# Two attention steps and a gated layer on one core: the first batch cut in seven chunks instead of eight, its 320-column chunk taken into the running maximum last, and a new instruction order

## The chip, the cores and the metric

The kernel runs on one core of one Trainium2 chip. The metric is the device time of one execution in microseconds (us). It was timed in 3 runs; the profile is of one more execution.

## What is computed

The input `x` has 4 batches of 12800 rows of 128 numbers. 32 inducing rows `I` first attend to `x`, which gives 32 rows `h` for each batch; then every row of `x` attends to `h`. The result goes through a causal convolution of 5 taps, whose sigmoid gates a linear map of it, and a second linear map.

```python
def mab(q, kv):
    s = scale * (q @ kv.transpose(0, 2, 1))
    s = s - s.max(-1, keepdims=True)
    a = np.exp(s)
    a /= a.sum(-1, keepdims=True) + 1e-09
    return a @ kv
h = mab(I, x)
attn = mab(x, h)
...
for k in range(K):                       # K = 5
    gate_pre += conv_w[k][None, None, :] * xp[:, k:k + S, :]
gate = 1.0 / (1.0 + np.exp(-gate_pre))
val = x @ w_val                          # x is attn here
return (gate * val @ w_out)
```

## The kernel before

The 12800 rows of a batch lie as 4 strips of 3200, and each strip is cut in chunks (`SIZES`), so that a chunk of 480 columns stands for 4 x 480 rows. A batch goes through two halves.

In the first half each chunk's scores against `I` are made (`s1`, L298, on PE) and moved to SBUF with their maximum (`e1`, L303, DVE). The maxima are merged in groups (`GROUPS`): `gm` (L320) reduces them, `ng` merges the four strips with five small operations (L335 and four of L337, on POOL or DVE), and `f` (L328, ACT) is the factor by which the older sums are scaled when the maximum has grown. Then the chunk's scores are exponentiated (`x1`, L345, ACT) and transposed (`tr`, L348, DVE), and PE adds them up against the rows of `x` (`h`, L362). DVE adds those sums (`ha`, L374 to L378) to `H`, and at the end PE and DVE turn `H` into `hT`, the 32 rows `h` (`hh`, L394 and L395; `hT`, L402 to L404).

`h` needs the rows of `x` in another layout (`xk`). For the later batches they are loaded; in the first batch most chunks (`MADE`) make them on the chip instead, by transposes on PE (`tp`, L272) that DVE or ACT copy to SBUF (`tpev`, L280 or L278).

The second half starts at `hT`. Its rows are folded into the weights of the gate and of the values (`g0` to `g3`, `wf`, `wt`, `W`; L412 to L472). A chunk is scored against `hT` (`s2`, L512, PE), transposed (`tin`, L516, DVE), and its softmax made: maximum (`mx`, L526, DVE), subtraction (`sub`, L531, POOL), exponential (`ex`, L537, ACT), sum and reciprocal (`sm`, L543 to L548, DVE), product (`nm`, L554, POOL), transposed back (`tout`, L557, DVE) and split in a high and a low half of 16 bits (`phi`, L560, ACT; `plo`, L562, POOL). Chunks that stand together in `JOINT` share these steps.

Then comes the `visit` of the chunk: PE's matmuls of 32 rows, four strips at once, 15 of the gate (L579) and 3 of the values (L586) for each strip. ACT takes the tanh (`th`, L671), DVE multiplies gate and values (`gv`, L680), ACT and POOL split the product in two halves of 16 bits (`hi`, L686, into a buffer `gh`; `lo`, L688, into a buffer `gl`), PE makes the output from these halves (`o`, L714, three matmuls for each of four strips), ACT or DVE move it to SBUF (`ev`, L726 or L728) and SP stores it. In the last chunk the output is made from 32-bit numbers.

What runs where and when is written out in three tables: `ORDER` lists all operations, each engine takes its own in that order, `SLOTS` gives each its buffer or PSUM bank, and `ENGINES` picks the engine of those that may run on two. The numbers next to an operation in the code (the costs) do not reach the chip; they are what the tables were once searched with. An engine runs in order, so an operation that waits holds all behind it.

`b`, `c`, `p` in a name are batch, chunk and pair of strips: `gv.0.1.0` is the first pair of chunk 1 of batch 0.

Of the kernel before, what the change touches and what calls it, by code (L numbers as in the profile page):

```python
# [35 lines left out]
SIZES = [[128, 256, 480, 480, 480, 480, 480, 416]] + [[448, 448, 448, 448, 448, 480, 480]] * 2 + [[448, 480, 480, 480, 480, 480, 352]]  # L36
XB = 15
JOINED = [[1], [], [], []]
CUTS = {(0, 2): [(0, 8), (8, 7)]}
MADE = {(0, 0): [], (0, 1): [], (0, 2): [], (0, 3): [], (0, 4): [], (0, 5): [], (0, 7): []}  # L40
GROUPS = [[[2, 3], [4, 5], [6, 7], [1, 0]]] + [[[0, 1, 2, 3], [4, 5, 6]]] * 3
HSUMS = [[[2, 3], [4, 5], [6, 7], [1, 0]]] + [[[0], [1], [2], [3], [4], [5], [6]]] * 3
JOINT = [[[0], [1], [2], [3], [4], [5], [6, 7]]] + [[[0], [1, 2], [3, 4], [5, 6]]] * 3
# [3 lines left out]
BUFS = dict(xt=10, xk=4, ss=5, et=3, e=2, pt=1, tg=4, gh=3, gl=2, os=4, H=2, z=3, m2=3, W=2, w2=2, wf=2, wo=2, wof=1, hT=2)  # L47
ASIDE = {(0, 0): 'os2', (0, 7): 'os2'}
# [46 lines left out]
def tile_kernel(ctx: ExitStack, tc: tile.TileContext, xt, xk, indT_in, w64, out):  # L95
# [7 lines left out]
    op = plan.op  # L103
# [4 lines left out]
    def tile_of(name, shape, dt=F32):  # L108
# [4 lines left out]
                  e=([P, 2 * XB, M], F32), pt=([P, 2 * CW], F32), tg=([P, 2, CW], F32), gh=([P, 2, CW], F16),  # L113
                  gl=([P, 2, CW], F16), os=([P, 2, CW], F32), H=([P, P + 1], F32), z=([P, 4, 32], F32),
# [14 lines left out]
        u=1, osc=1).items()} for b in range(B)]  # L129
# [182 lines left out]
    def group(b, g):  # L312
# [13 lines left out]
        op(("ng", b, g), ("POOL", "DVE"), f, dict(POOL=1.7, DVE=0.65), [("e1", b, cs[0]) if one else ("gm", b, g)])  # L326
        if g:
            op(("f", b, g), "ACT", lambda: S.activation(sm["f"][:, g:g + 1], sm["ng"][:, g - 1:g], AF.Exp, bias=sm["ng"][:, g:g + 1],  # L328
                                                        scale=-1.0), 0.22, [("ng", b, g), ("ng", b, g - 1)])
# [58 lines left out]
    def prep(b):  # L388
# [17 lines left out]
        op(("hT", b), "DVE", f_n, 0.62, [("hh", b)], [hT], [key])  # L406
# [42 lines left out]
        op(("g3", b), "DVE", g3, 0.48, [("g2", b), ("whi", b)], [], [pv, w2])  # L449
# [38 lines left out]
        op(("u", b), ("POOL", "DVE"), o1, dict(POOL=2.0, DVE=0.78), [("qm", b)])  # L488
# [318 lines left out]
def run_plan(tc, plan, slot):  # L807
# [173 lines left out]
```

## Time and profile before

| what | value |
| --- | --- |
| median of 3 runs (lowest, highest) | 277.88 us (277.62 to 278.01) |
| the profiled execution, its own time | 278.09 us |
| its span, first to last instruction | 276.3 us |
| PE busy (matmuls) | 263.6 us, 95% |
| DVE, ACT, POOL busy | 216.2, 202.0, 199.9 us |
| granted clock of PE | 1.000 of full speed |
| chain that ended last: PE, DVE, POOL | 72%, 14%, 6% of the span |

The profiled execution is 0.21 us above the median. PE is busy nearly all the time, but busy says only that a matmul is open; how dense its work is must be read from the rows of single stretches. The chain is followed back from the last instruction, each time to what released it.

### The profile page before, as it was taken

Reading aid. Unit: us, or ns where it says so; the run is one execution under the profiler, and the core shown is the slowest. Engines: PE = TensorE matmul, PEld = TensorE weight load, DVE = VectorE, ACT = ScalarE, POOL = GpSimd, SP = SyncE. Lnnn points to the kernel's source line nnn. Section 1 sums busy time; section 2 is a strip of 40 time slices with the busy share of each in tenths; the row PEclk is TensorE's granted clock in tenths of the full one; section 3 lists DMA queues with packets and bytes.
Section 4 is the critical chain, followed back from the end, with each engine's and each line's share of the span. In section 5 each row is a group of like instructions: output and inputs, shape, how many; then the busy total and the mean of one; then the engine's idle time right before and its main releaser. Section 6 shows DMA issues by size and latency. Waiting matters only on the chain.

```text
span 276.3 us, 10610 instructions
## 1 busy us (share of the span) xinstructions
PE 263.6 (95%) x4569; PEld 146.5 (53%) x4569; DVE 216.2 (78%) x455; ACT 202.0 (73%) x259; POOL 199.9 (72%) x182
## 2 busy tenths in 40 slices
PE   8999898798999999999999999999999999999993
PEld 4558336474444555665565476565445555444451
DVE  0669999997997999998786899887898953645561
ACT  2538257665568888676988685997598899997752
POOL 1002158766889948677998769999999999996650
PEclk9999999999999999999999999999999999999999
DMA  7999999679989599999996799443331443333466
GB/s 268 423 414 420 414 386 354 254 266 421 375 295 332 179 321 334 342 345 362 407 354 215 278 327 365 187 163 125 134 138 66 161 180 147 140 140 142 156 228 224
DMA packets 23631, 74.49 MB, mean 270 GB/s; under 512 B 1952, under 2 KB 16800, under 8 KB 23584
## 3 DMA queue, kind: packets, MB, share of 16 engines
q1 hardware_dynamic: 23440, 73.79, 71.4%
q8 instruction: 36, 0.59, 0.8%
q14 instruction: 11, 0.09, 0.1%
q10 hardware_dynamic: 144, 0.02, 0.0%
HBM read 47.58 MB, written 26.21 MB: 267 GB/s over the span
## 4 chain that ended last, share of the span: by engine, by line
PE 72%; DVE 14%; POOL 6%; issue 4%; ACT 2%; POOLq 0%; DVEq 0%; ACTq 0%
PE banks L579 24%; PE banks L714 21%; PE banks L362 7%; PE banks L298 5%; PE banks L586 5%; PE banks L512 5%; POOL gl L688 3%; DVE tg L680 2%; PE banks L272 2%; DVE ss L303 2%; PE banks L201 1%; DVE pt L557 1%; DVE ng L337 1%; DVE et L348 1%; DVE z L543 1%
## 5 line engine op out<-in xcount | busy, mean ns | idle before, releaser
L688 POOL TENSOR_TENSOR gl<-tg,gh 128x960 f16<-128x960 f32 (+4 forms) x56 | 104.8, 1882 | 23.2 <-PE banks L714 12.0
L579 PE MATMUL banks<-P,W 32*128 32x480 f16 (+5 forms) x1740 | 104.6, 345 | 0.9 <-ACT tg L671 0.5
L680 DVE SCALAR_TENSOR_TENSOR tg<-tg,banks 128x960 f32<-128x960 f32 (+5 forms) x58 | 61.6, 1064 | 28.5 <-ACT tg L671 24.1
L579 PEld LDWEIGHTS <-W 32*128 32x128 f16 x1740 | 53.4, 92 | 42.4 <-issue 13.7
L686 ACT CAST gh<-tg 128x960 f16<-128x960 f32 (+4 forms) x56 | 52.3, 933 | 21.7 <-PE banks L714 12.3
L714 PE MATMUL banks<-gh,wo 128*32 128x448 f16 (+6 forms) x584 | 63.5, 346 | 0.0
L671 ACT ACTIVATE tg<-banks,gsc 128x960 f32<-128x960 f32 (+5 forms) x58 | 55.1, 993 | 11.0 <-PE banks L579 9.3
L714 PEld LDWEIGHTS <-wo 128*32 128x32 f16 (+1 forms) x876 | 36.1, 97 | 36.2 <-issue 14.9
L728 ACT ACTIVATE os<-banks,osc 128x960 f32<-128x960 f32 (+4 forms) x43 | 41.1, 961 | 6.4 <-PE banks L714 5.6
L714 PE MATMUL banks<-gl,wo 128*32 128x448 f16 (+6 forms) x292 | 43.5, 346 | 1.7 <-issue 1.7
L586 PE MATMUL banks<-P,W 32*128 32x480 f16 (+5 forms) x348 | 41.5, 347 | 0.1
L362 PE MATMUL banks<-xk,et 128*32 128x129 f32 x800 | 27.8, 275 | 2.4 <-DVE tg L680 1.0
L554 POOL TENSOR_TENSOR e<-e,z 128x480 f32<-128x480 f32 (+5 forms) x19 | 25.3, 1335 | 4.3 <-ACT tg L671 1.5
L562 POOL TENSOR_TENSOR P<-pt,P 128x480 f16<-128x480 f32 (+5 forms) x19 | 28.2, 1484 | 0.1
L362 PEld LDWEIGHTS banks<-xk,et 128*32 128x32 f32 x800 | 23.7, 109 | 7.5 <-DVE tg L680 2.1
L531 POOL TENSOR_TENSOR e<-e,m 128x480 f32<-128x480 f32 (+5 forms) x19 | 25.2, 1335 | 2.2 <-DVE m L526 2.1
L298 PE MATMUL banks<-xt,indT 128*32 128x480 f32 (+2 forms) x208 | 25.1, 555 | 0.5 <-ACT xk L278 0.3
L512 PE MATMUL banks<-xt,hT 128*32 128x480 f32 (+2 forms) x208 | 25.3, 557 | 0.2 <-DVE tg L680 0.2
L726 DVE TENSOR_SCALAR os<-banks,osc 128x960 f32<-128x960 f32 (+4 forms) x21 | 19.9, 958 | 5.5 <-PE banks L714 3.7
L303 DVE TENSOR_SCALAR_CACHE_REDUCE ss<-banks 128x480 f32<-128x480 f32 (+5 forms) x29 | 17.5, 605 | 8.6 <-PE banks L298 8.4
L345 ACT ACTIVATE ss<-ss,ng 128x480 f32<-128x480 f32 (+5 forms) x29 | 17.2, 653 | 5.5 <-DVE ng L337 3.7
L516 DVE STREAM_TRANSPOSE e<-banks 128x480 f32<-128x480 f32 (+5 forms) x29 | 18.0, 630 | 1.2 <-PE banks L512 0.8
(104 smaller groups left out, 264.2 us busy)
## 6 DMA issues: line engine op xcount, KB each, us to landing
xt<-in_xt_dram SPq DMA_DIRECT2D x16, 960.0 KB, 8.7
out_dram<-os SPq DMA_DIRECT2D x28, 480.0 KB, 3.6
xk<-in_xk_dram SPq DMA_DIRECT2D x11, 904.0 KB, 8.7
out_dram<-os SPq DMA_DIRECT2D x22, 448.0 KB, 3.3
xk<-in_xk_dram SPq DMA_DIRECT2D x10, 968.0 KB, 8.2
xt<-in_xt_dram SPq DMA_DIRECT2D x8, 896.0 KB, 9.8
os<-in_xt_dram SPq DMA_DIRECT2D x1, 832.0 KB, 11.6
out_dram<-os SPq DMA_DIRECT2D x2, 416.0 KB, 6.2
```

Of the source, the lines that this page charges most:

```text
L298: T.matmul(buf(key)[32 * r:32 * r + 32, :n], c_["indT"], x[:, :, r, :], start=True, stop=True)
L362: T.matmul(buf(key)[32 * s:32 * s + 32, :P + 1], buf(("et", b, c))[:, 32 * i:32 * i + 32], buf(("xk", b, c))[:, i, :], start=j < R, stop=j ...
L512: T.matmul(buf(key)[32 * r:32 * r + 32, :n], buf(("hT", b)), x[:, :, r, :], start=True, stop=True)
L562: lambda: G.tensor_tensor(c_["P2"][:, o:o + n], buf(qk)[:, :n], c_["P1"][:, o:o + n], ALU.subtract), ("lo", n),
L579: T.matmul(buf(("ps2", "g", b, c, r // 2))[:, r % 2, :n], buf(("W", b))[q, w, k, :], c_[("P1", "P2")[e]][q, o:o + n], start=u == 0, stop=u ...
L586: T.matmul(buf(("ps2", "v", b, c, r // 2))[:, r % 2, :n], buf(("W", b))[q, w, TAPS, :], c_[("P1", "P2")[e]][q, o:o + n], start=u == 0, sto ...
L671: op(("th", b, c, p), "ACT", lambda: S.activation(buf(tg)[:, :, :n], buf(g)[:, :, :n], AF.Tanh, scale=small[b]["gsc"]), ("act", 2 * n, 0.0 ...
L680: V.scalar_tensor_tensor(t, t, 1.0, buf(v)[:, :, :n], ALU.add, ALU.mult)
L686: op(("hi", b, c, p), "ACT", lambda: S.copy(buf(g1)[:, :, :n], buf(tg)[:, :, :n]), ("act", 2 * n), [("gv", b, c, p)], [g1], [tg])
L688: lambda: G.tensor_tensor(buf(g2)[:, :, :n], buf(tg)[:, :, :n], buf(g1)[:, :, :n], ALU.subtract), ("lo", 2 * n),
L714: T.matmul(t[s], w[:, s], x, start=j == 0, stop=j == len(terms) - 1)
L728: S.activation(o, a, AF.Copy, scale=small[b]["osc"])
```

## The change

The first batch has seven chunks, 320 and six times 480, in place of eight (128, 256, five times 480, 416). The chunk of 320 is chunk 0. As before, the first chunk is loaded and scored late: the running maximum goes over the chunks in the order 1 and 2, 3 and 4, 5 and 6, 0, where it was 2 and 3, 4 and 5, 6 and 7, 1 and 0. Chunks 5 and 6 share one softmax (960 columns). The load of the first chunk is no longer shared with the next one's buffer. There are four buffers `gh` instead of three, and three `gl` instead of two. Some costs are set higher, and the three tables are new in full.

```diff
-SIZES = [[128, 256, 480, 480, 480, 480, 480, 416]] + [[448, 448, 448, 448, 448, 480, 480]] * 2 + [[448, 480, 480, 480, 480, 480, 352]]
+SIZES = [[320, 480, 480, 480, 480, 480, 480]] + [[448, 448, 448, 448, 448, 480, 480]] * 2 + [[448, 480, 480, 480, 480, 480, 352]]
-JOINED = [[1], [], [], []]
-CUTS = {(0, 2): [(0, 8), (8, 7)]}
-MADE = {(0, 0): [], (0, 1): [], (0, 2): [], (0, 3): [], (0, 4): [], (0, 5): [], (0, 7): []}
-GROUPS = [[[2, 3], [4, 5], [6, 7], [1, 0]]] + [[[0, 1, 2, 3], [4, 5, 6]]] * 3
+JOINED = [[], [], [], []]
+CUTS = {(0, 1): [(0, 8), (8, 7)]}
+MADE = {(0, 0): [], (0, 1): [], (0, 2): [], (0, 3): [], (0, 4): [], (0, 6): []}
+GROUPS = [[[1, 2], [3, 4], [5, 6], [0]]] + [[[0, 1, 2, 3], [4, 5, 6]]] * 3
...
-JOINT = [[[0], [1], [2], [3], [4], [5], [6, 7]]] + [[[0], [1, 2], [3, 4], [5, 6]]] * 3
+JOINT = [[[0], [1], [2], [3], [4], [5, 6]]] + [[[0], [1, 2], [3, 4], [5, 6]]] * 3
-BUFS = dict(xt=10, xk=4, ss=5, et=3, e=2, pt=1, tg=4, gh=3, gl=2, os=4, H=2, z=3, m2=3, W=2, w2=2, wf=2, wo=2, wof=1, hT=2)
-ASIDE = {(0, 0): 'os2', (0, 7): 'os2'}
+BUFS = dict(xt=10, xk=4, ss=5, et=3, e=2, pt=1, tg=4, gh=4, gl=3, os=4, H=2, z=3, m2=3, W=2, w2=2, wf=2, wo=2, wof=1, hT=2)
+ASIDE = {(0, 0): 'os2', (0, 6): 'os2'}
...
-        op(("ng", b, g), ("POOL", "DVE"), f, dict(POOL=1.7, DVE=0.65), [("e1", b, cs[0]) if one else ("gm", b, g)])
+        op(("ng", b, g), ("POOL", "DVE"), f, dict(POOL=1.75, DVE=1.1), [("e1", b, cs[0]) if one else ("gm", b, g)])
...
 ORDER = [
-    1, 0, 2, 19, 16, 20, 21, 22, 23, 25, 17, 24, 18, 33, 32, 52, 3, 136, 34, 141, 35, 133, 135, 62, 36, 134,
...
+    1, 0, 2, 18, 16, 19, 20, 21, 22, 23, 24, 3, 17, 31, 30, 50, 128, 127, 32, 129, 58, 131, 126, 33, 133, 59,
...
```

Which engine takes the five small operations of `ng` and of the similar `u` (the scale of the output) changes too: POOL runs 9 such groups instead of 7 (in the first batch `ng.0.0` is now on POOL; `ng.1.1` and `ng.2.1` as well, and `u.2` went to DVE). Of the 12 copies `tpev` of the first batch DVE makes 6 instead of 2.

Three places show what the tables move. The first is PE at the end of the first half of batch 0, from the last sums `h` to the first scores `s2`. Before:

```order
L362 MATMUL banks<-xk_114,et_79 32x129 x13
L362 MATMUL banks<-xk_111,et_77 32x129 x15
L362 MATMUL banks<-xk_112,et_78 32x129 x8
L362 MATMUL banks<-xk_114,et_79 32x129 x4
L394 MATMUL banks<-pick,H_92 128x32
L395 MATMUL banks<-pick,H_92 128x32
L298 MATMUL banks<-xt_67,indT 32x448 x4
L512 MATMUL banks<-os,hT_109 32x160 x4
```

And now, at the same place:

```order
L362 MATMUL banks<-xk_114,et_79 32x129 x15
L362 MATMUL banks<-xk_113,et_78 32x129 x15
L362 MATMUL banks<-xk_116,et_77 32x129 x10
L298 MATMUL banks<-xt_68,indT 32x448 x4
L394 MATMUL banks<-pick,H_94 128x32
L395 MATMUL banks<-pick,H_94 128x32
L298 MATMUL banks<-xt_69,indT 32x448 x4
L512 MATMUL banks<-os,hT_111 32x352 x4
```

One chunk of the second batch's scores (L298, 448 columns) now stands ahead of `hh`, and one behind it as before; the first `s2` has 352 columns instead of 160.

The second place is POOL in the second half of batch 0, from the scale of the output (L486) to the first low half of a product (`gl`). Before:

```order
L486 TENSOR_SCALAR osc_143<-u_142 128x1
L531 TENSOR_TENSOR e_81<-e_81,m_97 128x480
L562 TENSOR_TENSOR P_123<-pt_82,P_122 128x480
L531 TENSOR_TENSOR e_80<-e_80,m_98 128x480
L554 TENSOR_TENSOR e_81<-e_81,z_94 128x480
L498 TENSOR_TENSOR wo_106<-wof_108,wo_106 128x128
L688 TENSOR_TENSOR gl_90<-tg_83,gh_87 128x2x256
```

And now:

```order
L486 TENSOR_SCALAR osc_145<-u_144 128x1
L531 TENSOR_TENSOR e_80<-e_80,m_101 128x480
L562 TENSOR_TENSOR P_125<-pt_82,P_124 128x480
L531 TENSOR_TENSOR e_81<-e_81,m_99 128x480
L554 TENSOR_TENSOR e_80<-e_80,z_98 128x480
L554 TENSOR_TENSOR e_81<-e_81,z_96 128x480
L498 TENSOR_TENSOR wo_108<-wof_110,wo_108 128x128
L562 TENSOR_TENSOR P_125<-pt_82,P_124 128x480
L531 TENSOR_TENSOR e_80<-e_80,m_100 128x480
L335 TENSOR_SCALAR n_148<-m_147 64x1
L337 TENSOR_SCALAR ng_149<-n_148 32x1 x4
L688 TENSOR_TENSOR gl_91<-tg_84,gh_87 128x2x320
```

Between the two, POOL now works off nine operations instead of five, among them the second batch's second maximum (L335, L337), which was on DVE.

The third place is PE at the end of the program. Before, the last output of chunk 5 (`gh_89` and `gl_90`) stands between the first 32-bit output of chunk 6 (`tg_86`) and the other three:

```order
L586 MATMUL banks<-P_123,W_101 128x352
L714 MATMUL banks<-tg_86,wof_108 128x352
L714 LDWEIGHTS wo_107
L714 MATMUL banks<-gh_89,wo_107 128x480
...
L714 MATMUL banks<-gl_90,wo_107 128x480
L714 MATMUL banks<-tg_85,wof_108 128x352 x2
L714 MATMUL banks<-tg_86,wof_108 128x352
```

And now:

```order
L586 MATMUL banks<-P_124,W_103 128x352
L586 LDWEIGHTS W_103
L586 MATMUL banks<-P_125,W_103 128x352
...
L714 MATMUL banks<-tg_83,wof_110 128x352 x2
L714 MATMUL banks<-tg_84,wof_110 128x352 x2
```

The last output of chunk 5 now comes ahead of the last values (L586), and the four 32-bit outputs end the program without a break.

## Rows read from the trace of the kernel before

**Rows 1.** The page, its first part: busy time and share of PE.

```profile
PE 263.6 (95%) x4569; PEld 146.5 (53%) x4569; DVE 216.2 (78%) x455; ACT 202.0 (73%) x259; POOL 199.9 (72%) x182
```

**Rows 2.** Windows from 66 us on: busy us and instructions of each engine, clock, DMA.

```profile
core 0: us, PE busy (x) PEld busy (x) DVE busy (x) ACT busy (x) POOL busy (x), PEclk, DMA share, GB/s
66.00:110.00 44.00, 43.85 (x789) 22.05 (x784) 40.28 (x84) 35.04 (x43) 35.65 (x24) 1.00 0.88 314
...
190.00:215.00 25.00, 24.92 (x480) 11.86 (x472) 21.61 (x38) 20.32 (x25) 23.89 (x22) 1.00 0.31 113
...
sum 202.00, PE 201.62 PEld 108.10 DVE 162.03 ACT 163.99 POOL 172.22; mean PE 40.32 PEld 21.62 DVE 32.41 ACT 32.80 POOL 34.44
```

**Rows 3.** The chain, steady stretch at the end: start us, us, what.

```profile
243.27 2.44 PE banks L579 x48
246.31 2.54 PE banks L714 x12
249.57 2.44 PE banks L579 x48
```

**Rows 4.** Windows of 10 us in the head, same columns as rows 2.

```profile
30.00:40.00 10.00, 8.81 (x152) 3.65 (x156) 9.44 (x40) 2.90 (x6) 4.19 (x9) 1.00 0.99 392
40.00:50.00 10.00, 9.26 (x211) 5.59 (x204) 9.73 (x29) 6.93 (x13) 8.78 (x18) 1.00 0.94 370
50.00:60.00 10.00, 8.59 (x206) 6.00 (x204) 9.79 (x27) 7.68 (x14) 6.79 (x8) 1.00 0.59 209
```

**Rows 5.** Timeline of PE in the head: start us, us, what [idle before <- releaser].

```profile
38.65 0.68 PE L579 MATMUL banks<-P,W 32*128 32x128 f16 x20
...
41.01 0.84 PE L579 MATMUL banks<-P,W 32*128 32x128 f16 x42
...
50.72 1.98 PE L579 MATMUL banks<-P,W 32*128 32x480 f16 x33 [0.42 <-DVE ss L303]
...
54.86 0.96 PE L362 MATMUL banks<-xk,et 128*32 128x129 f32 x26 [0.99 <-DVE tg L680]
...
63.46 0.29 PE L714 MATMUL banks<-gl,wo 128*32 128x256 f16 x4 [1.66 <-issue]
...
65.01 0.36 PE L579 MATMUL banks<-P,W 32*128 32x480 f16 x2
...
67.13 0.41 PE L394 MATMUL banks<-pick,H 128*128 128x32 f32 x2
```

**Rows 6.** Timeline of DVE in the head.

```profile
11.93 0.86 DVE L337 TENSOR_SCALAR ng<-n 32x1 f32<-32x1 f32 x4
...
16.60 1.22 DVE L280 COPY xk<-banks 128x1024 f32<-128x1024 f32 x1
...
31.80 0.19 DVE L404 TENSOR_TENSOR hT<-banks,zz 128x32 f32<-128x32 f32 x1
...
43.08 1.76 DVE L348 STREAM_TRANSPOSE et<-ss 128x448 f32<-128x448 f32 x3
...
65.22 2.22 DVE L680 SCALAR_TENSOR_TENSOR tg<-tg,banks 128x960 f32<-128x960 f32 x2 [0.21 <-PE banks L586]
```

**Rows 7.** Timeline of POOL in the head.

```profile
25.35 1.62 POOL L337 TENSOR_SCALAR ng<-n 32x1 f32<-32x1 f32 x4
...
40.99 1.35 POOL L337 TENSOR_SCALAR ng<-n 32x1 f32<-32x1 f32 x4
...
67.53 2.01 POOL L688 TENSOR_TENSOR gl<-tg,gh 128x960 f16<-128x960 f32 x1 [2.49 <-ACT gh L686]
```

**Rows 8.** Timeline of all engines at the end.

```profile
267.02 0.61 PE L586 MATMUL banks<-P,W 32*128 32x352 f16 x6
...
269.47 2.17 PE L714 MATMUL banks<-tg,wof 128*128 128x352 f32 x6
...
270.78 0.30 PEld L714 LDWEIGHTS banks<-tg,wof 128*128 128x128 f32 x2 [0.53 <-ACT os L728]
...
272.12 0.41 ACT L728 ACTIVATE os<-banks,osc 128x176 f32<-128x176 f32 x1 [0.79 <-DVE os L726]
```

More of the change, by code (lines that the diff above doesn't have):

```diff
@@ L34 @@
 TRANSFERS = 1
-SIZES = [[128, 256, 480, 480, 480, 480, 480, 416]] + [[448, 448, 448, 448, 448, 480, 480]] * 2 + [[448, 480, 480, 480, 480, 480, 352]]
+SIZES = [[320, 480, 480, 480, 480, 480, 480]] + [[448, 448, 448, 448, 448, 480, 480]] * 2 + [[448, 480, 480, 480, 480, 480, 352]]
 XB = 15
-JOINED = [[1], [], [], []]
-CUTS = {(0, 2): [(0, 8), (8, 7)]}
-MADE = {(0, 0): [], (0, 1): [], (0, 2): [], (0, 3): [], (0, 4): [], (0, 5): [], (0, 7): []}
-GROUPS = [[[2, 3], [4, 5], [6, 7], [1, 0]]] + [[[0, 1, 2, 3], [4, 5, 6]]] * 3
-HSUMS = [[[2, 3], [4, 5], [6, 7], [1, 0]]] + [[[0], [1], [2], [3], [4], [5], [6]]] * 3
-JOINT = [[[0], [1], [2], [3], [4], [5], [6, 7]]] + [[[0], [1, 2], [3, 4], [5, 6]]] * 3
+JOINED = [[], [], [], []]
+CUTS = {(0, 1): [(0, 8), (8, 7)]}
+MADE = {(0, 0): [], (0, 1): [], (0, 2): [], (0, 3): [], (0, 4): [], (0, 6): []}
+GROUPS = [[[1, 2], [3, 4], [5, 6], [0]]] + [[[0, 1, 2, 3], [4, 5, 6]]] * 3
+HSUMS = [[[1, 2], [3, 4], [5, 6], [0]]] + [[[0], [1], [2], [3], [4], [5], [6]]] * 3
+JOINT = [[[0], [1], [2], [3], [4], [5, 6]]] + [[[0], [1, 2], [3, 4], [5, 6]]] * 3
 LATE = {(b, c, 0) for b in range(4) for c in range(len(SIZES[b]))} | {(0, 0, 1), (3, len(SIZES[3]) - 1, 1)}
@@ L324, in f @@
             over_strips(ENG[e], src, sm["n1"][:2 * M, g:g + 1], sm["ng"][:, g:g + 1], ALU.mult, -SCALE)
-        op(("ng", b, g), ("POOL", "DVE"), f, dict(POOL=1.7, DVE=0.65), [("e1", b, cs[0]) if one else ("gm", b, g)])
+        op(("ng", b, g), ("POOL", "DVE"), f, dict(POOL=1.75, DVE=1.1), [("e1", b, cs[0]) if one else ("gm", b, g)])
         if g:
             op(("f", b, g), "ACT", lambda: S.activation(sm["f"][:, g:g + 1], sm["ng"][:, g - 1:g], AF.Exp, bias=sm["ng"][:, g:g + 1],
-                                                        scale=-1.0), 0.22, [("ng", b, g), ("ng", b, g - 1)])
+                                                        scale=-1.0), 0.285, [("ng", b, g), ("ng", b, g - 1)])
         for c in cs:
@@ L404, in f_n @@
             V.tensor_tensor(buf(hT), t[:, :M], sm["zz"], ALU.mult)
-        op(("hT", b), "DVE", f_n, 0.62, [("hh", b)], [hT], [key])
+        op(("hT", b), "DVE", f_n, 0.79, [("hh", b)], [hT], [key])
         w2, wf, W = ("w2", b), ("wf", b), ("W", b)
@@ L447, in g3 @@
             V.scalar_tensor_tensor(w[:, 1, TAPS], p, vs, w[:, 0, TAPS], ALU.mult, ALU.subtract)
-        op(("g3", b), "DVE", g3, 0.48, [("g2", b), ("whi", b)], [], [pv, w2])
+        op(("g3", b), "DVE", g3, 0.53, [("g2", b), ("whi", b)], [], [pv, w2])
         def f8():
@@ L486, in o1 @@
             ENG[e].tensor_scalar(sm["osc"], sm["u"], 0.5 / SP / SO, None, ALU.mult)
-        op(("u", b), ("POOL", "DVE"), o1, dict(POOL=2.0, DVE=0.78), [("qm", b)])
+        op(("u", b), ("POOL", "DVE"), o1, dict(POOL=2.03, DVE=1.29), [("qm", b)])
         def o2():
```

162 rows, old and new, of tables (ENGINES, ORDER, SLOTS) are left out of this document.

## Prediction

> **What bounds the kernel now.** I read first the busy times, then windows over the span, then the timeline of PE. PE is busy 95% of the span [rows 1], but that alone only says that matmuls were open. The windows divide the program in two. From 66 us to 268 us PE is busy 201.62 of 202 us [rows 2], and the chain of the steady stretch at the end shows what such time is worth [rows 3]: 48 gate matmuls in 2.44 us are 50.8 ns each, so four strips of 480 columns take 203 ns, 2.36 columns a ns at a granted clock of 1.00; twelve full-height output matmuls in 2.54 us, 0.21 us each, say the same. So this part is work of PE and hardly anything else, and no order of the other engines makes it shorter by more than a few tenths per visit.
>
> Before 66 us it is different. There DVE is busy 9.44 to 9.79 of every 10 us, and PE waits [rows 4]: first gate matmuls at 38.65 us, the first of 480 columns going on at 50.72 after a wait for an `e1`, another wait of 0.99 us for a `gv` at 54.86, and one of 1.66 us for a low half of a product at 63.46 [rows 5]. From 65.01 us, when the gates of the fourth chunk start, PE runs on without a break. **So the whole time is: when the fourth chunk's gates start, how much of PE's fixed work lies behind them by then, and what follows the last matmul.** I compare the two kernels at that place and at the end.
>
> **Prices.** Sixty gate matmuls of 480 columns take 3.05 us, 6.35 ns a column of the chunk; twelve of the values 1.27 ns a column; the outputs 2.54 us per 480, 5.3 ns a column [rows 3]. A group of maxima costs 1.1 us on DVE (0.86 for four of its five operations) and 2.0 or 1.75 us on POOL (1.62 or 1.35 for the four) [rows 6, 7]. A copy of eight blocks is 1.22 us, a transposition of 448 columns 0.59, a `gv` of 960 numbers 1.11 [rows 6], a `lo` 2.01 [rows 7]; others I scale by their columns.
>
> **To `hT`: nothing gained.** In before DVE finishes `hT` at 32.0 us [rows 6]. The new order gives DVE four copies more and takes one group of maxima from it, but the first two copies fall where it idled. Walking through the queues with these durations, the maxima of chunks 5 and 6 are known some 0.5 us earlier than those of 6 and 7 were; then DVE still has the 320 columns of chunk 0, and the last group of maxima starts on POOL at the same 25 us as in before. Its exponential, transposition and sums are 0.1 to 0.2 us longer for 320 columns than for 256 and 128. `hT` comes at 32.3 us. PE has one `s1` of batch 1 more behind it (0.75 us).
>
> On the move of a group from DVE to POOL, the rows show 1.62 us for its four operations beside two-input work of DVE, and 1.35 us otherwise [rows 7]. The Trainium skill warns in "Perfetto Trace Analysis" (Optimizing Scalar/DVE Operations) that GPSIMD and DVE share an SBUF read port, so that offloading between the two might not help. That agrees with the 0.27 us; by it the two groups moved in the later batches would cost POOL 2.0 each and give DVE less than 1.1 back, by the rows 1.75 to 2.0. The sum is the same either way, as long as POOL has the time.
>
> **From `hT` to the first gates: 2.5 us later.** The first chunk has 352 columns to bring through DVE, POOL, ACT, POOL and back (160 in before), and four `e1` of batch 1 and the second chunk's `tin` and maximum stand between on DVE. I get 39.6 us for `tout` and 41.1 for `phi`, so gates from 41.1 us instead of 38.65. Against that the 60 matmuls behind it are 320 columns wide, not 128.
>
> **The next three chunks: earlier.** The second visit has already 480 columns. It needs three transpositions of batch 1 and a `tout` on DVE (44.8), the `phi` (45.5), and a PSUM bank that one more `e1` frees (46.0): 46.0 us. In before the first 480-column visit was held until 50.72. The third visit waits for banks that `th.0.1.1` (52.9) and then two `gv` of 640 numbers free: 53.6 us. Then come 3.6 us of visit, two `s2`, four `h`, three outputs' halves and `hh`. In this part I find one long wait: `o.0.1.0` needs the `lo` that POOL, after the nine operations, ends at 60.7, about 1 us after PE could start it. The fourth chunk's gates start at **67.2 us**.
>
> **Behind PE at that point.** Before, at 65.0: gates and values of 864 columns (128, 256, 480), outputs of 320 (chunk 1, half of chunk 0). After, at 67.2: gates of 1280, outputs of 560 (chunk 0, half of chunk 1), and `hh.1`, which in before cost 0.55 us at 67.13 [rows 5]. More is done by 416 x 6.35 ns = 2.64, 416 x 1.27 = 0.53, 240 x 5.3 = 1.27 and 0.55 us; less 0.39, since narrow gates were dear (42 of 128 columns in 0.84 us, 20 ns each where 13.5 would be their share [rows 5]), and that loss is gone in both reckonings. Together 4.6 us of work for 2.2 us of time: **2.4 us ahead**.
>
> **The buffers.** One more `gh` and `gl` let ACT and POOL run ahead; PE does not wait for them from 66 us on, so I cost this at nothing there. If that cover is missing, it is a gain, below.
>
> **The end.** In before the last values end at 267.63 and the last evacuation at 272.53 us, 4.9 us; in these PE makes an output of chunk 5 (1.25 us) and four 32-bit outputs, of which the last waits 0.53 us [rows 8]. Now the output of chunk 5 comes ahead, the four follow on each other at some 0.6 us, and the last evacuation adds 0.45 with its wait: 3.1 us. 4.9 - 1.25 - 3.1 leaves a gain of **0.5 us**. The last store is as large as before.
>
> **Sum.** Against the profiled execution's 278.09: -2.4 - 0.5, and +0.4 for short waits that a walk with bare durations leaves out: 275.6. The median of the runs lies 0.21 lower: **275.4 us**. The walk is the weak part. If every hand-over between engines costs 0.1 us more than I took, and some 20 of them stand one behind the other, the lead is 0.4; if the wait for the `lo` does not come, it is 3.4. So the likeliest case has 274.0 to 277.2.
>
> **The rivals.**
> - *DVE takes it all back (0.14).* It is full between 20 and 60 us in both kernels [rows 4], and one chunk fewer saves it only a few small instructions. Then the lead is 0 to 0.4, and only the end gains: 277.5 us. For it speaks the share of DVE; against it, that the work that DVE has before the fourth visit now serves 416 columns more.
> - *POOL makes the packed part wait (0.14), slower.* From 190 to 215 us POOL is busy 23.89 of 25 us [rows 2]. The new tables put two groups of maxima more on POOL (1.75 to 2.0 us each), in batches 1 and 2, ahead of `lo`s that PE's outputs need. If POOL is not ahead of PE where they stand, PE waits for nearly the whole 2 us at each, and the third boundary, where its load is highest, adds as much. It decides from 2.9 us of such waits in total; three of 2 us less the 2.9 are 3.1 us: 280.0 us is the far end, 279.0 the middle. Against it: PE never waited in this stretch before, and with three `gl` a `lo` can be made earlier.
> - *The packed part shrinks too (0.10).* If busy PE hides gaps between kinds of matmuls, a new order and one visit less could save there. Steady visits take 6.3 us [rows 3] against 3.05 + 0.61 + 2.54 = 6.2 us by the prices: 0.1 us each for 28 visits. With the extra buffers I allow 1.8 us: 273.6. In a sentence of its own: the Trainium skill's "Perfetto Trace Analysis" (Identifying the Most-Contended Engine) says that matmul busy time is not a good measure of how close PE is to its roofline, which is the rule that speaks for this rival; the 2.36 columns a ns above show that here the trace bears it out only by a few per cent.
>
> **How the numbers follow.** Forecast 0.62, DVE 0.14, POOL 0.14, packed part 0.10. About 0.2%, 0.56 us, is what a measurement of this kernel can tell from no change. Faster holds the forecast (its slow edge is 277.2, against 277.3), the packed part and a little of the DVE case: 0.74. The rest of that case is the same: 0.12. Slower is POOL: 0.14. The range takes in the DVE case and the packed part, and leaves out most of the POOL case and the far edges: 273.6 to 278.0.
>
> **What would show it.** In the new profile: `hT` near 32.3 us; gates of 320 columns from about 41, of 480 from about 46 and 53.6; the fourth chunk's first gate matmuls (480 columns, right after the small L394 and L395) near 67.2; `hh.1` ahead of them; from there PE again without breaks; the four 32-bit outputs at the end without the 0.53 us wait. The prediction is wrong if the second half of the head comes late (third visit after 56 us), if PE shows waits for POOL's L688 or DVE's L680 after 70 us, or if the visits' pace at the end is not 6.3 us.

## The result, and the profile after

The changed kernel takes 270.83 us (median of 4, 270.72 to 271.71) against 277.76 us; the ratio is 0.9756, with an interval of 0.9734 to 0.9778. That is 6.9 us faster, where 2.5 were forecast and the range ended at 273.6. The profiled execution, 271.71 us with a span of 269.7, is the longest of the four; the others have spans of 268.6 to 268.7. It has one wait of PE of 0.72 us at 118 us, which a profile of a kernel with the same tables from there on (hh_first, below) has not. The page of the changed kernel, its first part, answers to [rows 1]:

```profile
PE 261.9 (97%) x4505; PEld 143.5 (53%) x4505; DVE 215.9 (80%) x437; ACT 197.5 (73%) x248; POOL 201.8 (75%) x185
```

PE is busy 1.7 us less than before, so 4.9 of the 6.6 us of span were time in which PE did nothing. The windows, in the columns of [rows 2, 4]:

```profile
30.00:40.00 10.00, 8.67 (x131) 3.37 (x132) 9.58 (x35) 3.24 (x7) 5.69 (x12) 1.00 0.93 349
40.00:50.00 10.00, 9.94 (x219) 6.70 (x222) 9.39 (x25) 7.30 (x13) 8.43 (x15) 1.00 1.02 416
50.00:60.00 10.00, 9.76 (x188) 5.87 (x188) 9.72 (x19) 8.98 (x13) 9.01 (x11) 1.00 0.78 301
...
66.00:110.00 44.00, 44.00 (x816) 22.54 (x811) 41.54 (x89) 33.94 (x41) 36.01 (x29) 1.00 0.93 338
...
190.00:215.00 25.00, 25.00 (x464) 12.32 (x456) 20.58 (x35) 21.73 (x26) 23.81 (x17) 1.00 0.30 112
```

From 40 us on PE is nearly full (9.94 and 9.76 of 10 us), where it was full from 66 us before; DVE is as full there as it was, and the clock is 1.00 in both. From 10 to 20 us, ahead of [rows 4], DVE was not full before and now is; first the kernel before, then the changed one:

```profile
10.00:20.00 10.00, 9.68 (x137) 6.65 (x138) 7.42 (x22) 4.15 (x5) 0.25 (x2) 1.00 1.02 418
10.00:20.00 10.00, 10.00 (x145) 7.23 (x147) 9.32 (x25) 5.46 (x8) 1.68 (x7) 1.00 1.02 417
```

The longest of DVE's waits there before, and there is none like it in the changed kernel:

```profile
16.37 0.29 DVE L374 COPY H<-banks 128x129 f32<-128x129 f32 x1 [1.55 <-PE banks L362]
```

What PE waited for from 4 to 66 us (total us, times, longest), first in the kernel before:

```profile
PE banks L714 <- issue: 1.7, 1, 1.7
PE banks L362 <- DVE tg L680: 1.0, 1, 1.0
PE banks L394 <- DVE H L376: 0.6, 1, 0.6
PE banks L362 <- DVE et L348: 0.6, 2, 0.3
PE banks L362 <- ACT xk L278: 0.5, 1, 0.5
PE banks L579 <- ACT tg L671: 0.5, 1, 0.5
...
```

and in the changed one, all of it:

```profile
PE banks L298 <- DMA xt<-in_xt_dram: 0.9, 2, 0.6
PE banks L463 <- DVE w L447: 0.6, 1, 0.6
PE banks L579 <- ACT W L472: 0.4, 1, 0.4
PE banks L586 <- DVE H L378: 0.2, 1, 0.2
```

The first list comes to 6.5 us with its five smaller rows, the second to 2.1. The places of [rows 5, 6] in the new timelines of PE and DVE:

```profile
28.81 0.41 PE L394 MATMUL banks<-pick,H 128*128 128x32 f32 x2
...
30.05 0.96 PE L298 MATMUL banks<-xt,indT 128*32 128x448 f32 x8 [0.61 <-DMA xt<-in_xt_dram]
...
39.30 0.31 PE L579 MATMUL banks<-P,W 32*128 32x320 f16 x3
...
43.83 3.57 PE L579 MATMUL banks<-P,W 32*128 32x480 f16 x60
...
52.38 2.75 PE L579 MATMUL banks<-P,W 32*128 32x480 f16 x48
...
63.91 0.41 PE L394 MATMUL banks<-pick,H 128*128 128x32 f32 x2
64.15 0.39 PE L395 MATMUL banks<-pick,H 128*128 128x32 f32 x2
64.47 0.38 PE L579 MATMUL banks<-P,W 32*128 32x480 f16 x2
```

```profile
30.27 0.19 DVE L404 TENSOR_TENSOR hT<-banks,zz 128x32 f32<-128x32 f32 x1
```

`hT` is 1.5 us earlier than before, and the fourth chunk's gates start at 64.47, 0.54 us earlier, with 416 columns more of gates and values, 240 more of outputs and `hh.1` (64.15 in L395) done: 2.64 + 0.53 + 1.27 + 0.55, some 5.0 us of work. That makes a lead of 5.5 us by the prices. By the traces it is 202.6 us from the fourth chunk's gates to the end of the last values before, and 198.7 in the changed kernel, where an output of 1.25 us more stands in that stretch: 5.15 us, in spite of the wait at 118 us. The chain of the steady stretch answers to [rows 3]:

```profile
242.33 2.44 PE banks L579 x48
...
245.37 2.54 PE banks L714 x12
...
248.62 2.43 PE banks L579 x48
```

A visit of 480 columns takes 6.29 us, as before. At the end, against [rows 8]:

```profile
262.58 0.61 PE L586 MATMUL banks<-P,W 32*128 32x352 f16 x6
263.12 2.99 PE L714 MATMUL banks<-tg,wof 128*128 128x352 f32 x8
```

From the last values' end to the end of the span it is 269.7 - 263.19 = 6.5 us, before 276.3 - 267.63 = 8.7, of which 1.25 is the output that now stands ahead.

### The profile page after: what moved, and what is told of

Read it like the earlier page. It is cut to its first block, busy times and chain, and to the rows that moved or that the text cites. A ratio compares the mean times of both kernels' runs of the same rounds, so it can differ in the third digit from the quotient of the medians.

```text
span 269.7 us, 10436 instructions
## 1 busy us (share of the span) xinstructions
PE 261.9 (97%) x4505; PEld 143.5 (53%) x4505; DVE 215.9 (80%) x437; ACT 197.5 (73%) x248; POOL 201.8 (75%) x185
## 4 chain that ended last, share of the span: by engine, by line
PE 81%; DVE 10%; POOL 5%; issue 2%; ACT 1%; POOLq 0%; ACTq 0%
PE banks L579 30%; PE banks L714 25%; PE banks L512 7%; PE banks L362 6%; PE banks L586 6%; PE banks L298 5%; DVE ss L303 2%; PE banks L201 1%; POOL ng L337 1%; POOL e L531 1%; DVE et L348 1%; PE banks L272 1%; PE banks L463 1%; DVE xk L280 1%; POOL P L562 1%
## 5 line engine op out<-in xcount | busy, mean ns | idle before, releaser
L688 POOL TENSOR_TENSOR gl<-tg,gh 128x960 f16<-128x960 f32 (+2 forms) x54 | 104.4, 1947 | 11.0 <-PE banks L714 6.8
L579 PE MATMUL banks<-P,W 32*128 32x480 f16 (+3 forms) x1680 | 103.2, 351 | 0.6 <-ACT W L472 0.4
L680 DVE SCALAR_TENSOR_TENSOR tg<-tg,banks 128x960 f32<-128x960 f32 (+3 forms) x56 | 61.2, 1097 | 25.6 <-ACT tg L671 19.7
L686 ACT CAST gh<-tg 128x960 f16<-128x960 f32 (+2 forms) x54 | 51.6, 963 | 20.3 <-DVE tg L680 11.2
L714 PE MATMUL banks<-gh,wo 128*32 128x448 f16 (+4 forms) x600 | 63.2, 357 | 0.0
L671 ACT ACTIVATE tg<-banks,gsc 128x960 f32<-128x960 f32 (+3 forms) x56 | 54.7, 1021 | 11.6 <-PE banks L579 11.0
L714 PE MATMUL banks<-gl,wo 128*32 128x448 f16 (+4 forms) x300 | 43.4, 356 | 0.0
L728 ACT ACTIVATE os<-banks,osc 128x960 f32<-128x960 f32 (+3 forms) x43 | 41.3, 970 | 2.4 <-PE banks L714 2.4
L586 PE MATMUL banks<-P,W 32*128 32x480 f16 (+3 forms) x336 | 41.4, 353 | 0.2 <-DVE H L378 0.2
L562 POOL TENSOR_TENSOR P<-pt,P 128x480 f16<-128x480 f32 (+4 forms) x18 | 28.1, 1559 | 5.8 <-ACT P L560 5.7
L554 POOL TENSOR_TENSOR e<-e,z 128x480 f32<-128x480 f32 (+4 forms) x18 | 25.2, 1402 | 9.3 <-ACT tg L671 5.5
L298 PE MATMUL banks<-xt,indT 128*32 128x480 f32 (+2 forms) x208 | 25.2, 559 | 0.9 <-DMA xt<-in_xt_dram 0.9
```

The costliest lines, as they stand in the source:

```text
L298: T.matmul(buf(key)[32 * r:32 * r + 32, :n], c_["indT"], x[:, :, r, :], start=True, stop=True)
L562: lambda: G.tensor_tensor(c_["P2"][:, o:o + n], buf(qk)[:, :n], c_["P1"][:, o:o + n], ALU.subtract), ("lo", n),
L579: T.matmul(buf(("ps2", "g", b, c, r // 2))[:, r % 2, :n], buf(("W", b))[q, w, k, :], c_[("P1", "P2")[e]][q, o:o + n], start=u == 0, stop=u ...
L586: T.matmul(buf(("ps2", "v", b, c, r // 2))[:, r % 2, :n], buf(("W", b))[q, w, TAPS, :], c_[("P1", "P2")[e]][q, o:o + n], start=u == 0, sto ...
L671: op(("th", b, c, p), "ACT", lambda: S.activation(buf(tg)[:, :, :n], buf(g)[:, :, :n], AF.Tanh, scale=small[b]["gsc"]), ("act", 2 * n, 0.0 ...
L680: V.scalar_tensor_tensor(t, t, 1.0, buf(v)[:, :, :n], ALU.add, ALU.mult)
```

## The experiments

Times are medians; the ratio is to the kernel before, run beside it, with its interval. The rows of the tables are named by operations, in the order of one engine.

**The order before `hT`.** In the changed kernel PE scores the next two chunks ahead of the first sums. One run puts that back, one does it in the kernel before:

```diff
 h_first, PE and DVE of the changed kernel
-s1.0.3 s1.0.4 h.0.1 h.0.2         e1.0.3 e1.0.4 gm.0.1 ng.0.1 ha.0.1 tpev.0.3.8
+h.0.1 h.0.2 s1.0.3 s1.0.4         ha.0.1 tpev.0.3.8 e1.0.3 e1.0.4 gm.0.1 ng.0.1
 before_s1_early, PE and DVE of the kernel before
-h.0.2 h.0.3 tp.0.5.0 s1.0.5       ha.0.2 tpev.0.4.0 e1.0.5 gm.0.1 ng.0.1
+s1.0.5 h.0.2 h.0.3 tp.0.5.0       e1.0.5 gm.0.1 ng.0.1 ha.0.2 tpev.0.4.0
```

> The changed kernel (270.8 us) with one thing put back as it was before: in the first batch PE adds up the first two chunks (h) ahead of the scores (s1) of the next two, and DVE takes ha and a copy of eight blocks ahead of their maxima (e1). Theory (DVE is full until hT, so a wait of DVE there lengthens the program): the third chunk's e1 starts near 17.2 us instead of 14.24, 1.4 us of other DVE work is done meanwhile, hT comes 1.6 us later (near 32), the time is 272.4 (272.0 to 272.8). Rival (the gain comes from seven chunks and what lies behind PE at the fourth visit; the order before hT is immaterial): 270.8 plus or minus 0.3.

> The kernel before (277.8 us) with one part of the change alone: the scores of the fourth chunk it loads stand ahead of the first sums h on PE, and their maximum, the merge and the factors (e1, gm, ng) ahead of ha on DVE. Still eight chunks. Theory: DVE's waits of 1.55 and 0.54 us go away, hT comes near 30.4 instead of 32.0, the time is 276.2 (275.8 to 276.8). Rival (the chunks make the gain): 277.8 plus or minus 0.3.

h_first: 272.50 us, 0.9819 (0.9798 to 0.9839), 1.7 us slower than the changed kernel, as the theory had it; `hT` comes at 31.99. DVE's wait came back, and ahead of it one of PE, for the first transposition:

```profile
13.39 1.84 PE L362 MATMUL banks<-xk,et 128*32 128x129 f32 x58 [0.99 <-DVE et L348]
```

```profile
15.38 0.29 DVE L374 COPY H<-banks 128x129 f32<-128x129 f32 x1 [1.55 <-PE banks L362]
```

From 10 to 20 us PE is busy 8.67 and DVE 7.19 us. So the order is shown to matter, but not which of the two engines holds the other.

before_s1_early: 277.29 us, 0.9976 (0.9963 to 0.9988). `hT` comes at 31.04, 0.76 us earlier (0.27 of it the first load), half of what was expected; DVE's two waits went, but two of 0.66 and 0.63 us came in their place, and PE kept waits for copies of ACT and for `H`. The edit is worth 0.3 to 1.0 us.

**Is DVE the bound before `hT`?** Three runs on the changed kernel:

```diff
 conv_early: SP, DVE, and two copies
-xt.0.1 ... xt.0.6 raw              conv.0 to conv.10, wts between e1, tr and ha
+raw xt.0.1 ... xt.0.6              conv.0 to conv.10, wts, then e1.0.1
-tpev.0.1.0, tpev.0.1.8 on DVE
+tpev.0.1.0, tpev.0.1.8 on ACT
 pe_probe, in tp
+if (b, c, g) == (0, 4, 0):
+    for _ in range(6):
+        T.matmul(buf(tk)[:, 0, :], c_["zero"][:, :P], c_["zero"], start=True, stop=True)
 dve_probe, ahead of the transposition in tr
+if (b, c) == (0, 3):
+    V.memset(store["tg"][3], 0.0)
```

> The changed kernel with the 64-bit weights loaded first and their twelve conversion steps (conv, wts; about 4.1 us of DVE) moved from between the maxima and sums to DVE's idle time before 7 us; the first two copies go to ACT, which is idle. Theory in its plain form (DVE alone bounds the time to hT): the rows of x land 0.65 us later, DVE has 4 us less to do, hT comes 2.5 us earlier, 268.3. Rival (PE, busy 9.44 of 10 us from 20 to 30, and the loads of x are right behind DVE): hT 0.6 to 1 us earlier, 270.0. A further one: what comes after hT takes it back, 270.8.

> The changed kernel with six more matmuls of 128x512 on PE, of zeros, put ahead of the transposes of the fourth chunk (near 16 us); their results are overwritten. Five such matmuls at the start took 2.34 us, so six are some 2.6 us (1.3 if they run twice as fast there; the trace will tell). Theory formed after the first runs (from 4.6 us to the end PE has hardly a wait in the changed kernel, so what PE does ahead of hT counts in full): the time grows by all that they take, 2.0 to 2.8 us, to 273. Rival, as in my prediction (DVE bounds the time to hT and PE waits for it): the six hide, 270.8 to 271.3.

> The changed kernel with one memset of 128x960 numbers (about 1.0 us by the row of 128x256 in 0.27 us) more on DVE, ahead of the third transposition (tr) of the first batch near 18 us, into a buffer that is free. If DVE alone bounds the time to hT: +1.0 us, 271.8. If PE does and DVE is only close behind it: 0.3 to 0.7, 271.3. If DVE has slack: 270.8.

conv_early: 271.40 us, 0.9775 (0.9755 to 0.9794), no gain. DVE was rid of 4 us and waited instead. But with the weights loaded first the rows of `x` land later, and PE starts at 5.16 where the changed kernel starts at 4.55. PE's rows there, with `hh` nearly where it was (28.81):

```profile
5.16 1.94 PE L272 MATMUL banks<-identf,xt 128*128 128x128 f32 x8 [0.40 <-DMA xt<-in_xt_dram]
...
28.04 0.96 PE L298 MATMUL banks<-xt,indT 128*32 128x448 f32 x8
28.93 0.41 PE L394 MATMUL banks<-pick,H 128*128 128x32 f32 x2
```

So 0.5 us was made up before `hh`, and the run can't say what less work on DVE is worth by itself.

pe_probe: 271.71 us, 0.9788 (0.9756 to 0.982); the six matmuls took PE 1.3 us, of which 0.9 came out.

dve_probe: 271.48 us, 0.9788 (0.9751 to 0.9825), the memset took 0.86 us, of which 0.65 came out.

Both differences lie inside the intervals, but all six runs of each were above three of the four of the changed kernel. In both profiles the fourth gates start at 64.93, 0.46 us later than in the changed kernel; three profiles with the same order up to there (the changed kernel, packed_pool and tail_back, below) have them at 64.38 to 64.48. So about half of either addition reaches that place: neither engine has much slack before `hT`, and neither alone is shown to be the bound.

**More before `hT`, and behind it.**

```diff
 hh_first, changed kernel: PE and DVE (s1.1.1 with a bank of its own)
-s1.1.1 hh.0                        conv.10 ha.0.0 wts e1.1.1 hT.0 g0.0
+hh.0 s1.1.1                        ha.0.0 conv.10 wts hT.0 g0.0 e1.1.1
 before_head, kernel before: as before_s1_early, and ACT, DVE
-x1.0.1 x1.0.0 f.0.3 tpev.0.1.0     conv.9 ha.0.1
+tpev.0.1.0 x1.0.1 x1.0.0 f.0.3     ha.0.1 conv.9      (tpev.0.2.0 on DVE)
 u_late, changed kernel: POOL (u2.0 on DVE, wof.0 and woh.0 on ACT as far behind)
-u.0 sub.0.2 plo.0.1 sub.0.3 nm.0.2 nm.0.3 wol.0
+sub.0.2 plo.0.1 sub.0.3 nm.0.2 nm.0.3 u.0 ... wol.0
```

> The changed kernel with hT put ahead of what need not stand before it: one s1 of batch 1 behind hh on PE (with a bank of its own) and its e1 behind the first of the gate's scales, the last addition to H ahead of the last conversion step. PE's dense stretch from 4.6 us is then 0.75 us shorter up to hh. Theory (PE bounds the time to hT): hT 0.3 to 0.5 earlier; at the fourth gates no more than 0.3 is left, as PE has the same work up to there and waits only 2 us in all: 270.4 to 270.9. Rival (what stands between hT and the first gates sets the time): 270.0 or less.

> The kernel before, still eight chunks, with the first half of batch 0 put in order as far as a few moves do it: scores and maxima of the fourth loaded chunk ahead of the first sums (as in the run with that alone, which kept waits of PE of 0.40, 0.22, 0.54 and 0.58 us), the first copy on DVE, a late copy on ACT ahead of two exponentials, the third addition to H ahead of a conversion step. Theory (each wait of PE ahead of hT is time): hT near 30.2 instead of 31.8, the fourth chunk's gates near 63.4 instead of 65.0, the time 276.3 (275.9 to 276.8). Rival (only the chunks matter): 277.3 or more. What the changed kernel gains beyond it, some 5 us, would then be the chunks' and the second half's.

> The changed kernel with the output's scale u of the first batch (1.97 us on POOL from 41.4 us, which the chain of waits goes through) moved behind four later steps of POOL, and the three steps that follow from it (u2, wof, woh, then wol) moved as far. If what the chain shows there sets the time: the third visit's product comes up to 2 us earlier, 269.0 to 270.0. If PE, busy 9.94 of the 10 us from 40 to 50, is the bound: 270.8 plus or minus 0.4.

hh_first: 270.76 us, 0.9758 (0.9735 to 0.9781), the same as the changed kernel, though `hT` came at 29.37, 0.9 us earlier; PE waited longer for the rows of batch 1 (0.55 us at 34.63), and at the visits 0.3 us was left. A reason is in the row at 30.05 of the changed kernel: the `s1` of batch 1 that stands ahead of the first `s2` starts at 29.96 to 30.05 in five profiles (the changed kernel, conv_early, u_late, packed_pool, tail_back) whose `hT` comes at 29.97 to 30.27, and in three of them the wait is put down to the load of its rows. An earlier `hT` finds that load in its way.

before_head: 279.56 us, 1.0061 (1.0041 to 1.008), a miss: the copy put ahead of the exponentials made `H` late, and PE waited for it; `hT` came 0.46 us later than before, not 1.6 earlier, and from the first visit to the last every tanh stood 1.3 to 1.4 us later.

```profile
30.55 0.41 PE L394 MATMUL banks<-pick,H 128*128 128x32 f32 x2 [1.48 <-DVE H L376]
```

u_late: 273.32 us, 0.986 (0.9823 to 0.9897), a miss too, 2.5 us slower. On DVE `u2` now waits for `u`, and `ha` stands behind it; PE's timeline in that run:

```profile
51.61 0.56 PE L586 MATMUL banks<-P,W 32*128 32x320 f16 x9 [1.43 <-DVE H L378]
...
52.91 0.76 PE L586 MATMUL banks<-P,W 32*128 32x480 f16 x5 [0.40 <-DVE H L378]
```

Whether `u` alone costs anything on POOL this run can't say.

**The width of the first chunk.**

```diff
-SIZES = [[320, 480, 480, 480, 480, 480, 480]] + ...
+SIZES = [[448, 480, 480, 480, 480, 480, 352]] + ...
```

> The changed kernel with the same tables, but the first batch cut 448, five times 480, 352 instead of 320 and six times 480: still seven chunks, only the first is wider and the last narrower. If the small first chunk matters (its 352 columns go through the last merge, hT and the first softmax with nothing else for PE): hT 0.4 to 0.6 later, the first gates about 1.3 later, of which the first visit gives 0.8 back as more columns lie behind it: 271.3 to 272.0. If only the number of chunks matters: 270.8 plus or minus 0.3.

wide_first: 273.12 us, 0.9842 (0.981 to 0.9874), 2.3 us slower with the same tables. `hT` was as early (30.31), but the first gates came 1.5 us later and the second visit 2.3 (46.09); the fourth gates started at 67.66, 3.2 us later, with 128 columns more of gates, values and outputs behind them (1.7 us by the prices). That the first chunk is small is worth more than I thought, and seven chunks alone are not the gain; but the tables were made for a first chunk of 320 columns, and tables made for 448 were not tried.

**The wait of 1.66 us.** In [rows 5] it has no releaser. The narrow chunks' outputs stand there, many short matmuls. Four kernels made from the one before:

```diff
 before_warm4
-WARM = 8
+WARM = 4
 before_full_form (before_ff_s1: with the edit of before_s1_early)
-                o["fn"](forms[i])
+                o["fn"]("full" if o["name"][1:3] in ((0, 0), (0, 1)) else forms[i])
 before_even (before_even_s1: with the edit of before_s1_early)
+FORM = {("o", 0, c, q): "full" for c in (0, 1) for q in (0, 1)}
+FORM |= {("o", 0, 3, q): "strips" for q in range(4)}
-                o["fn"](forms[i])
+                o["fn"](FORM.get(o["name"], forms[i]))
```

> The kernel before with four matmuls instead of eight in the warm-up of PE: the stream of PE's instructions is eight shorter (four matmuls, four weight loads) and nothing else differs. It is to tell what the wait of 1.66 us at 61.8 us is, for which the trace has no releaser. If PE has run out of instructions (blocks of them come by a queue of their own): the wait stays, but four matmuls later in the program, behind the four of 256 columns that read gl. If it waits for the low half of the product: it stays right ahead of these four. Time as before, 277.2 to 278.5.

> The kernel before with the outputs of its two narrow chunks (128 and 256 columns) made by matmuls of the full height, 12 where there were 48, as the later chunks' are: the same products, PE's time for the columns the same by the prices, but 144 matmuls and 144 weight loads fewer in the stream between 56 and 63.5 us. Theory (PE ran out of instructions there): the wait of 1.66 us at 61.8 goes, the fourth chunk's gates start near 63.4 instead of 65.0, the time is 276.2 (275.9 to 276.7). Rival (the wait is for data, or it comes back in the next block): 277.6.

> That kernel with the scores and maxima of the fourth loaded chunk ahead of the first sums as well, which alone brought hT 0.8 us forward. If both are waits of PE that add up, fourth gates near 62.6, the time 275.4 (275.0 to 276.0), and what the changed kernel has beyond that, some 4.6 us with 1.3 of the end, is the seven chunks' and the second half's order. If the one takes the other's place: 276.2.

> The kernel before with four of the eight outputs of the narrow chunks (first pair of strips of chunks 0 and 1, right ahead of the wait at 61.8 us) made by 3 matmuls of the full height each where there were 12, and the four outputs of chunk 3 (near 84 us) by 12 where there were 3: 36 matmuls and 36 weight loads fewer at the one place and as many more at the other, the same products. (The run before_full_form, by this count, took away 72 and 72, not the 144 and 144 that I wrote.) Theory (PE ran out of instructions at 61.8): the wait goes or shrinks below 0.5 us, nothing new comes behind 84 us, the time is 276.3 (276.0 to 276.8). Rival (PE waits as long in all, wherever): 277.5 or more.

> The same, with the scores and maxima of the fourth loaded chunk ahead of the first sums, as in the run that brought hT 0.8 us forward. If the two add up: 275.5 (275.0 to 276.0), and some 4.7 us of the 6.9 are left to the seven chunks, the second half's order and the end. If the wait only moves: 276.5 to 277.5.

before_warm4: 278.87 us in its one run, its first load late. The wait stands four matmuls later, behind the `gl` of 256 columns; the releaser that the view names is a guess, DVE has nothing for that `h`:

```profile
62.50 0.28 PE L714 MATMUL banks<-gh,wo 128*32 128x256 f16 x2
62.61 0.28 PE L714 MATMUL banks<-gl,wo 128*32 128x256 f16 x2
64.31 1.08 PE L362 MATMUL banks<-xk,et 128*32 128x129 f32 x30 [1.42 <-DVE z L545]
```

So it hangs on the place in PE's stream of instructions, not on data. Two versions of the changed kernel have such a wait too: u_late (0.21 us) and packed_pool (0.51 us), at the same matmul, the 44th of the 60 sums of chunks 3 and 4, near 20.6 us; they are the two whose first load came earliest.

before_full_form: 279.54 us, 1.0076 (1.0052 to 1.0101), slower, though the wait was gone and the fourth gates started 1.85 us earlier (0.44 of it the first load). The gain held until 107 us; then PE waited anew, for nothing that the view can name (from 100 to 170 us; the wait of 0.3 ends at 108 us, that of 1.1 at 127):

```profile
PE banks L579 <- issue: 1.1, 1, 1.1
PE banks L714 <- issue: 0.3, 1, 0.3
PE banks L362 <- issue: 0.2, 1, 0.2
```

before_ff_s1 did the same, 278.69 us, 1.0051 (1.0029 to 1.0072).

before_even, with the stream behind 84 us where it was, is the clean test: 276.78 us, 0.9958 (0.9944 to 0.9972). Its PE has one wait of 0.19 us left there,

```profile
62.94 0.39 PE L588 MATMUL banks<-P,W 32*128 32x480 f16 x4 [0.19 <-issue]
```

its tanhs are 0.58 us earlier than before up to 54.8 us (its first load came earlier), 1.85 from 68.9 us on, and 1.8 at the last: 1.3 us, neither lost nor grown. before_even_s1: 276.10 us, 0.9932 (0.9918 to 0.9946); the two add up, less than was hoped.

**The packed part and the end.**

```diff
 packed_pool, changed kernel: lo made twice in six places
+TWICE = {(1, 1, 0), (1, 4, 0), (2, 1, 0), (2, 4, 0), (3, 1, 0), (3, 4, 0)}
 before_bufs
-gh=3, gl=2
+gh=4, gl=3
 tail_back, changed kernel: PE, and ev.3.5.1 from DVE to ACT (small copies and stores follow)
-o.3.5.2 o.3.5.3 visit.3.6.5 visit.3.6.6 o.3.6.0 o.3.6.1 o.3.6.2 o.3.6.3
+visit.3.6.5 visit.3.6.6 o.3.6.0 o.3.5.2 o.3.5.3 o.3.6.2 o.3.6.3 o.3.6.1
```

> The changed kernel with six of the low halves (lo, 2.0 us each on POOL) of batches 1 to 3 made twice, 12 us more of POOL's work between 100 and 260 us, where POOL is busy four fifths of the time and more. If PE bounds that part: less than 0.6 us, up to 271.4. If POOL does, or is as close as my rival had it (2 us of PE's wait at each place where POOL isn't ahead): 274 to 282.

> The kernel before with the four gh and three gl of the changed kernel and nothing else: every operation where it was, only the buffer numbers of gh and gl dealt out anew. My prediction's price for the buffers alone: nothing, 277.7 plus or minus 0.3. Rival (ACT and POOL run ahead and PE's last waits go): 276.5 to 277.3.

> The changed kernel with the end ordered as before: the output of the last chunk but one (second pair) stands behind the first 32-bit output, its copy on ACT, and the fourth 32-bit output is last. The prediction's term for the end: 0.5 us slower, 271.3. Read from the two traces (from the last values to the end of the last store 8.67 us before and 6.5 after, of which 1.25 is an output that only moved): 0.9 us slower, 271.7. Rival (the end is hidden): 270.8.

packed_pool: 277.58 us, 1.0004 (0.999 to 1.0019); of 12 us more on POOL 6.7 came out, and PE's waits name POOL:

```profile
PE banks L716 <- POOL gl L689: 3.0, 4, 1.4
```

POOL is close behind PE there; in the changed kernel no such wait is left. before_bufs: 277.38 us, 0.9991 (0.9977 to 1.0005), nothing. The opposite, the new tables with fewer buffers, was not tried.

tail_back: 272.07 us, 0.9808 (0.9786 to 0.983), 1.2 us slower, more than either reading. The stores of the last 7.7 us (KB each, median us to landing), in the changed kernel from 262 us on, and in the kernel before from 268.6:

```profile
out_dram<-os SPq DMA_DIRECT2D x4, 176.0 KB, 1.9
out_dram<-os SPq DMA_DIRECT2D x1, 480.0 KB, 2.7
```

```profile
out_dram<-os SPq DMA_DIRECT2D x4, 176.0 KB, 2.4
out_dram<-os SPq DMA_DIRECT2D x1, 480.0 KB, 2.7
```

With the output of chunk 5 early, its last store of 480 KB is further ahead of the last small ones (the copy for it starts 7.3 us before the end of the span, at 262.38, and 6.6 us before it in the kernel before, at 269.67), and these land in 1.9 us instead of 2.4. That the large store is the cause is read from these rows; no run parts it from the order of the copies.

## Why the prediction was wrong

The frame held: the time is when the fourth chunk's gates start, what lies behind PE by then, and the end; the packed part gave little, the buffers nothing, and no rival came. The numbers inside failed: the gates came 2.7 us before the forecast, 0.4 us more lay behind PE, the end gave 0.7 more, and the allowance of 0.4 was not needed, 4.2 of the 4.6 us by which the forecast was too slow.

- **"To `hT`: nothing gained", the step that failed first.** I walked through DVE's queue with bare durations, taking a full DVE for the bound, and got 32.3 us; it was 30.27 + 0.19. The rows that I had for a full DVE, [rows 4], begin at 30 us, when the first half is nearly over: from 10 to 20 us DVE was busy 7.42 of 10 us, and is 9.32 now. What the new order removes is waits of PE and DVE for each other and for the copies: 1.9 us on PE before `hh` is due (0.28, 0.32, 0.24, 0.52 and 0.58), none in the changed kernel, and on DVE 1.55 and 0.54. h_first, which brings waits of both back, loses 1.7 us. Which engine is the bound there stays open.
- **The wait of 1.66 us was misread.** I took it for a low half of a product, though the row says that PE waited for nothing the profile shows, and I put a similar wait of about 1 us for a `lo` into the new kernel. It hangs on PE's stream of instructions (before_warm4, before_even: 1.3 us, shown); the `lo` wait never came. Against the forecast `hT` was 1.8 us earlier, the first gates 1.8 (39.30 for 41.1), the second visit 2.2 (43.83 for 46.0) and the fourth gates 2.7 (64.47 for 67.2). The last 0.9 us came behind the first gates, where the `lo` wait of about 1 us had been put.
- **The work behind PE** was nearly right: 4.6 us forecast, 5.0 by the prices without the 0.39 that I took off for narrow gates, 5.15 by the traces.
- **The end** was mis-sized: 0.5 forecast, 1.2 measured (tail_back). The evacuations were counted, but not that the last small stores land 0.5 us sooner when the store of 480 KB is further ahead.
- **The allowance of 0.4 us** for short waits was not needed: a walk that is already too slow needs none. It is also in only some of the sums: with it the ends of the likeliest case are 274.4 and 277.4, not 274.0 and 277.2.
- **The rivals.** POOL had a real price (packed_pool), and its condition was not met; by its own sum its far end was 281.0 us, not 280.0. A steady visit did not shrink, 6.29 us. Still, behind 66 us some 0.2 us more was gained than the prices say (5.15 against 5.0), and hh_first, without the wait at 118 us, is 0.3 us ahead of the changed kernel's profile up to 112 us and 1.25 from 124 us on: so up to 1.1 us of the gain may lie in the packed part, against the 1.8 of that rival, and no run says where. DVE took nothing back.

If the parts add up, then of the 6.9 us 1.2 are the end, 1.1 to 1.3 the wait for instructions, and 0.3 to 1.7 the order before `hT` (by before_s1_early and h_first). Of the rest, 2.7 to 4.3 us, wide_first shows that with these tables a narrow first chunk matters by 2.3. How it divides between seven chunks and the order of the second half stays open: no kernel of eight chunks with a second half ordered anew was run. No version beat the changed kernel clearly.

## What to carry to other kernels

Where one engine is full for most of the time, add up its own waits in the part where it is not, by what ended them; a change is worth about what it takes off that list (here 4.4 of a lead of 5.5 us), and a neighbour's busy share must be read in the same stretch: DVE was full from 20 us on, but not from 10 to 20, where the order had something to gain. A wait that the profile can give no releaser for is no wait for data until shown: move the stream by a few instructions and look whether the wait moves along. At the end of a kernel look at the stores too, and at what is issued just ahead of the last one.

## What the runs showed of the hardware

PE can stop at a place that the data don't explain. With outputs of 128 and 256 columns, 32 matmuls between 60.86 and 61.80 us, it stood 1.66 us, at a place fixed by the count of instructions ahead; 144 instructions fewer there (72 matmuls and 72 weight loads) took that wait away and made others of 0.3 us at 108 us and of 1.1 at 127. That PE ran out of instructions there is inferred from this. The kernel before shows 36 packets of 0.59 MB in all on the queue of instructions,

```profile
q8 instruction: 36, 0.59, 0.8%
```

one of them from 61.20 to 62.16 us, where PE stops. The Trainium skill says in "Runtime: NRT & Kernel Launch" (Instruction fetch mechanics) that a sequencer fetches blocks of 16 KiB, 256 instructions, while it executes, and that the cost of a boundary is mostly hidden. The size of the packets agrees, and so does "mostly": in that profile one wait of 1.66 us stands against 36 packets. Whether the full DMA queues around it (a share of 1.02 from 60 to 66 us, and 1.02 again from 124 to 127 us in before_full_form) are needed for the wait was not tried.

The first load's landing differs by up to 1.0 us between executions (the first `e1` at 6.76 to 7.72 us in kernels that start alike). In the kernel before most of it comes out at the end: in before_warm4 the first `e1` is 0.96 us later and the last tanh 0.76. In the changed one it is taken up on the way: the fourth gates start at 64.38 us in packed_pool, whose first `e1` is at 6.77, and at 64.47 in the changed kernel, with 7.72.
